# Two rounds of cached attention and MLP on one core: the queries of sixteen heads as products of 512 columns, wq in a bank of its own, output projections in 320 columns

## The chip, the cores and the metric

The kernel runs on one core of a Trainium2 chip, in one launch. The metric is the time of the program on the device in microseconds. Before the change three runs gave 711.83, 711.88 and 713.04 us, so the median is 711.88 us. The profile is that of one further execution; its span, from the first to the last instruction, is 710.5 us.

## The reference

x has four rows (B = 4) of 640 columns. Two rounds of the same two layers are computed, with the same weights and the same caches both times:

```python
# W = 1024: only the last 1024 of 4096 cache positions are used
def _A_ref(x, k_cache, v_cache, wq, wo):
    q = (x @ wq).reshape(4, 1, 32, 128).transpose(0, 2, 1, 3)
    scores = einsum("bhqd,bhkd->bhqk", q, k) * 128 ** -0.5
    p = softmax(scores, axis=-1)
    o = einsum("bhqk,bhkd->bhqd", p, v)
    return o.transpose(0, 2, 1, 3).reshape(4, 1, 4096) @ wo
def _B_ref(x, w1, w2):                     # w1 640 x 1728, w2 1728 x 640
    return maximum(x @ w1, 0) @ w2
x = x + _A_ref(layernorm(x), ...);  x = x + _B_ref(layernorm(x), ...)
x = x + _A_ref(layernorm(x), ...);  x = x + _B_ref(layernorm(x), ...)
```

Everything is float32. Each head has its own K and V for each of the four batch rows, so a head of a round needs 4 MB of cache for four rows of queries.

## The kernel before, in words

A column here is one float32 in each of the 128 partitions, 512 bytes. The host lays out one record per head in `rec`: 640 columns of wq, 4096 of K, 4096 of V and 640 of wo, together REC = 9472 columns (L48 to L51). The on-chip memory holds five records (`slots`, NS = 5, L128) and a `ring` of 9152 columns (L130). The ring takes the MLP weights (`w`, 17,280 columns a round), and most of record 26 (SIXTH, L62) stays in it or passes through it.

**Loads.** SP issues all loads from one list, `items`, which is written out at L209 to L245. `pump` (L247) issues the next piece when no part of its place is still `live`; `done` (L278) frees a part after the last product that reads it, and calls `pump`. So the list is strictly in order: a piece whose place isn't free holds up all behind it, and the DMA engines work only on what was issued before. In the steady part five records are cut into three pieces of some 15,800 columns (`stream`, L191).

**Work on a head.** `query` (L377) makes five products for a head: a 128x128 block of wq is the stationary side, four columns of x (transposed, `xT`) the moving side, and the result, scaled by the layernorm's deviation, is `qT`. `scores` (L388) makes eight products of 512 columns, `softmax` and `weights` turn them into the stationary side of `values` (L408), eight more products of 512 columns. `picks` (VectorE) and `output_T` bring the head's output into `oTs`, and `project` (L441) makes four products of 160 columns with wo, one for each quarter of the output, into `acc`, which is the residual x itself.

**Order.** The main loop (L500) writes the instructions of each engine in the order in which they are issued; the helper InOrder (L80) keeps it, so that nearly all instructions carry the helper's line L94. In the step of index n, `scores` of head n+1, `values` of head n, the query of head n+2, `output_T` and `project` of head n follow each other on TensorE. Round 0 takes the heads 0 to 31; round 1 takes 27 to 31, which are still in the slots, then 26 from the ring, then 0 to 25. At the start of a round `center` (L337) transposes x, and the first head's query is made from x that isn't centered: `centered_wq` (L327) has subtracted the mean from head 27's wq during the MLP of round 0. `deviation` follows inside the first `scores`. The start of round 1 is where the list has small pieces (L226 to L239), since only a part of the memory is free.

Of the kernel before, what the change touches and what calls it, by code (L numbers as in the profile page):

```python
# [22 lines left out]
WQ, K, V, WO = 0, D, D + 4 * W, D + 8 * W  # L48
REC = 2 * D + 8 * W
HALF = REC // 2  # L50
VH = 2 * W  # L51

# [9 lines left out]
SIXTH = H - NS - 1  # L62
RING = WO + 2 * FD
W1_COLS = KB * FF
KEPT = 4 * FF + 32
LENT = 512
BESIDE = KEPT - 192 - (512 - FD)
HELD = BESIDE - LENT

MLP_RING = [(4, 0, 0), (4, 0, FF), (4, 0, 2 * FF), (4, 0, 3 * FF), (4, 0, 0), (0, 10, 1728), (0, 11, 3328), (0, 11, 5088),  # L70
            (0, 10, 0), (0, 8, 1600), (0, 4, 2880)]

SIXTH_PIECES = [(3520, 5088), (5088, HELD), (0, 1600), (1600, 3520)]
FILL = [False, False, False, True]
W1_SLOT = [[0, 1], [2], [3], [4]]
W2_SLOT = [22, 14, 10, 4, 4]
LATE = 5

# [23 lines left out]
def decode_kernel(ctx: ExitStack, tc: tile.TileContext, xf, rec, w, out):  # L102
# [15 lines left out]
    qT = sb.tile([P, B], F32, name="qT")  # L118
    of_batch = sb.tile([P, B], F32, name="of_batch")
    of_block = sb.tile([P, 4], F32, name="of_block")  # L120
    pick = sb.tile([P, B], F32, name="pick")
    by_row = sb.tile([P, 2 * B], F32, name="by_row")
# [5 lines left out]
    slots = sb.tile([P, NS * REC], F32, name="slots")  # L128
    slot = [slots[:, i * REC:i * REC + REC] for i in range(NS)]
    ring = sb.tile([P, RING], F32, name="ring")  # L130
# [5 lines left out]
    acc = ps.tile([P, 512], F32, name="acc")  # L136
    outs = [o_ps, sc_ps[0][:, 512:]]

    dve.memset(x_sb, 0.0)
    for n in range(NB):  # L140
        act.dma_start(x_sb[32 * n:32 * n + B], xf[B * n:B * n + B])
    ident = ring[:, :P]
# [13 lines left out]
    dve.tensor_reduce(pick, same[:, :32].rearrange("p (c j) -> p j c", j=4), op=OP.add, axis=AX.X)  # L156
    dve.memset(small, EPS)
# [7 lines left out]
    LAST = H - NS  # L165
    order = [list(range(H)), list(range(LAST, H)) + [SIXTH] + list(range(SIXTH))]

    def home(h, r):

        if h == SIXTH:  # L170
            return "ring"
        return h % NS if not r or h >= LAST else (h + LAST) % NS
# [3 lines left out]
    at = {("rec", 1, SIXTH): [(0, RING, "ring", 0), (RING, REC, "ring", 0)]}  # L176
    live = []
    buffers = {"slots": slots, "ring": ring}

    def place(buf, col):  # L180
        return (buf, col) if buf == "ring" else ("slots", buf * REC + col)

    def load(key, src, lo, hi, buf, col):
        buf, col = place(buf, col)
        items.append(([(key, lo, hi, col)] if key else [], src, lo, hi, buf, col))

    def piece(r, h, lo, hi, buf=None, col=None):
        buf, col = place(home(h, r) if buf is None else buf, lo if col is None else col)
        items.append(([(("rec", r, h), lo, hi, col)], rec, h * REC + lo, h * REC + hi, buf, col))

    def stream(r, h, cuts):  # L191

        assert [home(h + i, r) for i in range(NS)] == list(range(NS))
        for a, b in zip(cuts, cuts[1:]):
            parts = [(("rec", r, h + i), max(a - i * REC, 0), min(b - i * REC, REC), max(a, i * REC))
                     for i in range(NS) if a < i * REC + REC and i * REC < b]
            items.append((parts, rec, h * REC + a, h * REC + b, "slots", a))
# [12 lines left out]
    piece(0, hs[0], 0, V)  # L210
    piece(0, hs[0], V, REC)
    stream(0, 0, [REC] + CUTS[1:])
    for h in range(NS, 5 * NS, NS):
        stream(0, h, CUTS)
    for h in hs[5 * NS:-3]:
        piece(0, h, 0, RING if h == SIXTH else WO if h >= H - LATE else REC)
    piece(0, SIXTH, RING, REC, "ring", 0)
    ending(0, hs, True)
    n = 0
    for quarters, tiles, col in MLP_RING:  # L220
        size = quarters * FQ + tiles * FD
        load(("w", 0), w, n, n + size, "ring", col)
        n += size


    for lo, hi in SIXTH_PIECES:  # L226
        load(None, rec[:, SIXTH * REC:], lo, hi, "ring", lo)
    new = order[1][NS + 1:]
    for i, lo, hi in ((0, 0, K), (0, K, K + VH), (0, K + VH, V), (1, 0, K + VH), (1, K + VH, V), (0, V, V + VH),
                      (0, V + VH, REC), (2, 0, V), (1, V, REC), (3, 0, V), (2, V, REC), (4, 0, V), (3, V, REC),  # L230
                      (4, V, REC)):
        piece(1, new[i], lo, hi)
    for h in new[NS:-3]:
        if h >= 2 * NS - 2:
            if home(h, 1) == 0:
                stream(1, h, CUTS)
        else:
            piece(1, h, 0, REC)
    ending(1, new, False)  # L239
    for ks in W1_SLOT:  # L240
        load(("w", 1), w, ks[0] * FF, (ks[-1] + 1) * FF, "ring", ks[0] * FF)
    n = W1_COLS
    for size in W2_SLOT:
        load(("w", 1), w, n, n + size * FD, home(new[-5], 1), n - W1_COLS)
        n += size * FD  # L245
# [32 lines left out]
    def done(key, lo, hi):  # L278

        if key[0] == "rec" and key[1] == 0 and key[2] >= LAST:  # L280
            return
        if key == ("rec", 0, SIXTH):
            hi = min(hi, HELD)
# [6 lines left out]
    aside = acc[:, FD:], ring[:, BESIDE:BESIDE + 512 - FD]  # L290
    held = [(0, 0, REC - RING), (REC - RING, BESIDE + 512 - FD, KEPT)]
    lent = sc_ps[1][:, :LENT], ring[:, HELD:BESIDE]

    def put_by():

        for col, a, b in held:
            dve.tensor_copy(hold[:, col:col + b - a], ring[:, a:b])
            free("ring", a, b)
        free("ring", BESIDE, KEPT)
        pump()  # L300

    def lend():

        act.activation(*lent, AF.Copy)
        free("ring", HELD, BESIDE)
        pump()

    def take_back():

        assert not any(buf == "ring" and x < BESIDE and HELD < y for buf, x, y in live), live  # L310
        act.activation(*lent[::-1], AF.Copy)
        live.append(("ring", HELD, BESIDE))

    def put_back():

        for col, a, b in held:
            assert not any(buf == "ring" and x < b and a < y for buf, x, y in live), (a, b, live)
            dve.tensor_copy(ring[:, a:b], hold[:, col:col + b - a])
            live.append(("ring", a, b))
        live.append(("ring", BESIDE, BESIDE + 512 - FD))  # L320
# [6 lines left out]
    def centered_wq(h, ks):  # L327

        mean = sc_ps[1][:, 512:512 + DH]
        for k in ks:  # L330
            pe.matmul(mean, minus.to_broadcast([P, P]), cols(("rec", 0, h), WQ + k * DH, DH), start=(k == 0),
                      stop=(k == KB - 1))
        if ks[-1] == KB - 1:
            wq = cols(("rec", 0, h), WQ, D).rearrange("p (k d) -> p k d", d=DH)
            dve.tensor_tensor(wq, wq, mean.unsqueeze(1).to_broadcast([P, KB, DH]), op=OP.add)

    def center(key=None, fill=True):  # L337

        x = acc[:, :FD]
        if key:  # L340
            q = sc_ps[0][:, :B]
            dve.transpose(xT[:, :64], x[:, :64])
            dve.transpose(xT[:, 64:], x[:, 64:])
            dve.tensor_reduce(sums, x, op=OP.add, axis=AX.X)
            for k in range(KB):
# [250 lines left out]
```

## Time and the profile before

| | us |
|---|---|
| median of three runs | 711.88 |
| lowest, highest | 711.83, 713.04 |
| span of the profiled execution | 710.5 |
| TensorE busy with products | 513.6 |
| VectorE busy | 323.3 |
| ScalarE busy | 99.7 |

The profiled execution's own time isn't given beside its span; the median of the runs is 1.4 us above that span, and this difference is used as what lies around it. The page names work by the program's tiles: `slots<-rec` is a load of record columns into the slots, `sc_ps<-slots,qT` a product of scores, `o_ps<-slots,scratch` one of values, `acc<-slots,oTs` one of the output projection, `sc_ps<-xT,slots` one of a query. Each product is counted as two matmul rows and two weight-load rows (992 rows of scores for 62 heads with eight products each). In the chain of waits a line has its start, its length and what it is; a DMA line is the time from the issue of a load to the moment when work that waited for it could start.

### The profile page before, as it was taken

To read this page: it belongs to the slowest core of one execution; us is meant where nothing else is said; L and a number is where in the kernel's file an instruction comes from. 1 tells how busy PE (TensorE), PEld (TensorE's weight loads), DVE (VectorE), ACT (ScalarE), POOL (GpSimd) and SP (SyncE) were. 2 spreads that over 40 slices of the span, in tenths; PEclk is the share of its full clock that TensorE was granted. 3 is DMA by queue.
4 is the path that set the end of the run, shared out by engine and by line. 5 is a ranking of instruction groups with operands and counts; after the bars stand their busy time and mean duration, and the time that the engine had idled before them with its cause. 6 is when DMAs were issued, how large, how long until landed. Compare 5 with 4: busy or idle time off the path is not lost.

```text
span 710.5 us, 8690 instructions
## 1 busy us (share of the span) xinstructions
PE 513.6 (72%) x3706; PEld 202.8 (29%) x3706; DVE 323.3 (46%) x678; ACT 99.7 (14%) x211; POOL 1.1 (0%) x9
## 2 busy tenths in 40 slices
PE   3567686678584578857888898865686677576897
PEld 2132232232231223322223334331331322231423
DVE  3333353353452353546641777644352444253762
ACT  1100110011010110111121212201010111011111
POOL 0000000000000000000000000000000000000000
PEclk9957787677777776888999899977576677677899
DMA  9999999999999999999999999999999999999997
GB/s 381 463 409 451 415 442 443 414 442 444 424 429 440 434 429 421 435 425 430 424 416 403 421 435 428 438 434 448 429 445 427 428 442 430 427 442 406 431 423 292
DMA packets 13318, 302.64 MB, mean 426 GB/s; under 512 B 1488, under 2 KB 1760, under 8 KB 5216
## 3 DMA queue, kind: packets, MB, share of 16 engines
q1 hardware_dynamic: 13248, 302.08, 99.1%
q8 instruction: 29, 0.48, 0.2%
q14 instruction: 9, 0.07, 0.0%
q10 hardware_dynamic: 32, 0.01, 0.0%
HBM read 302.00 MB, written 0.08 MB: 425 GB/s over the span
## 4 chain that ended last, share of the span: by engine, by line
DMA 73%; PE 21%; DVE 4%; issue 1%; ACT 1%; SPq 0%; ACTq 0%; DVEq 0%
DMA slots<-rec 57%; PE sc_ps L94 11%; DMA ring<-w 8%; PE o_ps L94 7%; DMA ring<-rec 5%; PE acc L94 2%; DMA slots<-w 2%; DVE scratch L94 2%; DVE o_ps L94 1%; ACT oTs L94 1%; DVE small L94 0%; ACT sc_ps L94 0%; DVE turned L94 0%; SPq L94 0%; DVE ring L94 0%
## 5 line engine op out<-in xcount | busy, mean ns | idle before, releaser
L94 PE MATMUL sc_ps<-slots,qT 128*4 128x512 f32 x992 | 194.5, 869 | 37.4 <-DMA slots<-rec 36.4
L94 PE MATMUL sc_ps<-xT,slots 128*128 128x4 f32 x620 | 94.6, 279 | 99.8 <-DMA slots<-rec 99.2
L94 PE MATMUL o_ps<-slots,scratch 128*16 128x512 f32 x960 | 149.3, 693 | 2.4 <-DVE scratch L94 1.7
L94 DVE TENSOR_REDUCE small<-sc_ps 128x1 f32<-128x1024 f32 x64 | 78.3, 1224 | 156.9 <-PE sc_ps L94 156.9
L94 PEld LDWEIGHTS sc_ps<-xT,slots 128*128 128x128 f32 x620 | 89.2, 225 | 157.8 <-DMA slots<-rec 109.0
L94 ACT ACTIVATE sc_ps<-sc_ps,small 128x1024 f32<-128x1024 f32 (+1 forms) x68 | 71.1, 1046 | 342.2 <-DVE small L94 340.7
L94 DVE STREAM_TRANSPOSE turned<-sc_ps 128x1024 f32<-128x1024 f32 (+1 forms) x85 | 84.6, 996 | 0.7
L94 PEld LDWEIGHTS o_ps<-slots,scratch 128*16 128x16 f32 x960 | 34.5, 118 | 120.0 <-issue 107.6
L94 DVE TENSOR_TENSOR o_ps<-o_ps,of_block 128x512 f32<-128x512 f32 x62 | 43.4, 699 | 53.6 <-PE o_ps L94 52.3
L94 PEld LDWEIGHTS sc_ps<-slots,qT 128*4 128x4 f32 x992 | 32.3, 108 | 121.9 <-issue 64.9
L94 DVE TENSOR_TENSOR qT<-sc_ps,by_row 128x4 f32<-128x4 f32 x62 | 9.7, 156 | 114.1 <-PE sc_ps L94 114.1
L94 PE MATMUL acc<-slots,oTs 128*4 128x160 f32 x496 | 35.4, 368 | 19.2 <-ACT oTs L94 18.5
L94 DVE TENSOR_REDUCE scratch<-o_ps 128x128 f32<-128x512 f32 x62 | 42.9, 691 | 2.1
L94 ACT ACTIVATE oTs<-o_ps 128x4 f32<-128x4 f32 x64 | 11.1, 174 | 214.1 <-PE o_ps L94 214.1
L94 PE MATMUL o_ps<-pick,scratch 128*128 128x4 f32 x128 | 26.8, 280 | 15.9 <-DVE scratch L94 15.9
L94 PEld LDWEIGHTS o_ps<-pick,scratch 128*128 128x128 f32 x128 | 22.4, 218 | 21.4 <-DVE scratch L94 21.1
L94 DVE TENSOR_TENSOR scratch<-turned,by_row 128x128 f32<-128x128 f32 (+1 forms) x85 | 22.0, 259 | 3.2
L94 PE MATMUL sc_ps<-slots,small 128*1 128x512 f32 (+2 forms) x56 | 21.5, 486 | 0.0
L94 DVE TENSOR_SCALAR by_row<-of_batch,small 128x4 f32<-128x4 f32 x64 | 14.7, 230 | 2.2
L94 PEld LDWEIGHTS acc<-slots,oTs 128*4 128x4 f32 x496 | 6.9, 84 | 25.2 <-ACT oTs L94 23.5
L94 DVE STREAM_TRANSPOSE scratch<-small 128x32 f32<-128x32 f32 x64 | 12.9, 202 | 2.2 <-ACT sc_ps L94 2.2
L94 ACT ACTIVATION_READ_ACCUMULATOR sc_ps<-sc_ps,small 128x1 f32 x64 | 12.3, 193 | 0.0
(66 smaller groups left out, 103.7 us busy)
## 6 DMA issues: line engine op xcount, KB each, us to landing
slots<-rec SPq DMA_DIRECT2D x15, 7872.0 KB, 27.0
slots<-rec SPq DMA_DIRECT2D x8, 7936.0 KB, 31.5
slots<-rec SPq DMA_DIRECT2D x17, 2368.0 KB, 16.9
slots<-rec SPq DMA_DIRECT2D x4, 4736.0 KB, 25.9
slots<-rec SPq DMA_DIRECT2D x2, 4416.0 KB, 29.3
slots<-rec SPq DMA_DIRECT2D x7, 1024.0 KB, 19.7
ring<-w SPq DMA_DIRECT2D x8, 864.0 KB, 10.9
ring<-rec SPq DMA_DIRECT2D x1, 4576.0 KB, 36.2
```

The costliest lines, as they stand in the source:

```text
L94: r = build(*args, **kwargs)
```

## The change

- wq leaves the records. REC is 8832 columns: K, V, wo. An array `wq` of two halves of 10,240 columns holds sixteen heads each; on the chip a half goes to `bank`, a tile of 10,240 columns. The slots get 1728 columns more (`extra`, from E0 on), the ring is gone, and the MLP weights of round 0 pass through `extra` and the fifth slot; those of round 1 go to the bank and the slots.
- `batch` makes the queries of sixteen heads: 20 products in which five columns of xT (four rows of x and one of ones) are the stationary side and 512 columns of wq the moving side. `turn` transposes the result on VectorE and applies mean and deviation. One batch stands at the start of each round, in `begin`, which replaces the first `center`; the other half's batch stands after the step of index 9 in round 0 and of index 3 in round 1 (BATCH). `query` and `centered_wq` are gone. The half that is used last in round 0 stays in the bank for the start of round 1; the other is loaded again.
- In 27 of 32 steps of round 0 and 24 of round 1, `project_wide` makes two products of 320 columns in place of four of 160. They go to `acc2`, and the last of a round adds it to `acc`.
- Round 1 takes 28 to 31, then 27 (FIFTH, of which a part stays in the fifth slot), then 0 to 26. Its list of loads after the small pieces goes on with the large pieces of `stream` at once, where there were three pieces of one record each before.

The loads, counted from the lists, are 589,824 columns before and 589,952 now, in as many DMAs.

```diff
-WQ, K, V, WO = 0, D, D + 4 * W, D + 8 * W
-REC = 2 * D + 8 * W
+K, V, WO = 0, 4 * W, 8 * W
+REC = 8 * W + D
+NQ = H // 2
+QB = KB * NB * 512
+LAST = H - NS + 1
+FIFTH = LAST - 1
+WIDE = [range(0, 27), range(4, 28)]
+BATCH = [9, 3]
...
-    ring = sb.tile([P, RING], F32, name="ring")
+    bank = sb.tile([P, QB], F32, name="bank")
...
+    queries(0, 0, 0, QB, "bank", 0)
+    stream(0, 0, [0, REC + V + 512, 3 * REC])
+    stream(0, 3, CUTS)
+    queries(0, 1, 0, QB, "bank", 0)
...
+    for i, j in ((3, 7), (7, 15), (15, 20)):
+        queries(1, 0, 512 * i, 512 * j, "bank", 512 * (i - 3))
...
-    for h in new[NS:-3]:
-        if h >= 2 * NS - 2:
-            if home(h, 1) == 0:
-                stream(1, h, CUTS)
-        else:
-            piece(1, h, 0, REC)
+    for h in (5, 10, 15):
+        stream(1, h, CUTS)
...
+    def batch(r, i, q, ks):
+        key = ("wq", r, i)
         for k in ks:
+            for j in range(NB):
+                pe.matmul(q[32 * j:32 * j + B + 1, :], xT[:, 32 * k:32 * k + B + 1], cols(key, 512 * (NB * k + j), 512),
+                          start=(k == 0), stop=(k == KB - 1))
+            done(key, 2048 * k, 2048 * k + 2048)
+
+    def turn(i, q, a, b):
+        dve.transpose(t_ps[:, 32 * a:32 * b], q[:, 32 * a:32 * b])
+        t = t_ps.rearrange("p (h j) -> p h j", j=32)[:, a:b]
+        n = b - a
+        dve.tensor_tensor(shift[:, a:b], t[:, :, B:B + 1].to_broadcast([P, n, B]),
+                          means.unsqueeze(1).to_broadcast([P, n, B]), op=OP.mult)
+        dve.tensor_tensor(qT[:, i, a:b], t[:, :, :B], rstds.unsqueeze(1).to_broadcast([P, n, B]), op=OP.mult)
+        dve.tensor_tensor(qT[:, i, a:b], qT[:, i, a:b], shift[:, a:b], op=OP.add)
+
+    def begin(r):
+        x, q, i = acc[:, :FD], sc_ps[1][:, 512:], r
+        dve.transpose(xT[:, :64], x[:, :64])
+        dve.transpose(xT[:, 64:], x[:, 64:])
+        dve.tensor_reduce(sums, x, op=OP.add, axis=AX.X)
+        batch(r, i, q, range(1))
+        pe.matmul(o_ps[:, :B], sums.to_broadcast([P, P]), first_rows, start=True, stop=True)
+        square(centered)
+        batch(r, i, q, range(1, 3))
+        deviation(eps_dh, float(DH))
...
+        batch(r, i, q, range(3, KB))
+        a = order[r][0] % NQ
+        turn(i, q, a, a + 2)
...
+    def project_wide(r, h, n):
+        key = ("rec", r, h)
+        for g in range(2):
+            pe.matmul(acc2[32 * g:32 * g + B, :], oTs[:, 0], cols(key, WO + g * (D // 2), D // 2),
+                      start=False, stop=(n == WIDE[r][-1]), skip_group_check=True)
...
-            query(r, hs[n + 2], n % 2)
             output_T(max(i, 0))
-            if i < 0:
+            if n in WIDE[r]:
+                project_wide(r, h, n)
+            elif i < 0:
                 project(r, h, 0, False)
...
+            if n == BATCH[r]:
+                batch(r, 1 - r, hold, range(KB))
+                turn(1 - r, hold, 0, NQ)
```

The first place is TensorE's start of round 1. Before, the last products of the MLP (`acc<-ring,scratch`) are followed by the query of head 27 and by its scores, with the mean and the deviation (`o_ps<-...small`) between them, and then by the first steps:

```order
L94 MATMUL acc<-ring,scratch 4x160 x12
L94 MATMUL sc_ps_72<-xT,slots 128x4 x5
L94 MATMUL o_ps<-pick,small 128x4
L94 MATMUL sc_ps_72<-slots,qT 4x512 x4
L94 MATMUL o_ps<-small 128x4
L94 MATMUL sc_ps_72<-slots,qT 4x512 x4
L94 MATMUL sc_ps_73<-xT,slots 128x4 x5
L94 MATMUL sc_ps_73<-slots,qT 4x512 x8
L94 MATMUL o_ps<-slots,scratch 16x512 x8
L94 MATMUL sc_ps_72<-xT,slots 128x4 x5
L94 MATMUL o_ps<-pick,scratch 128x4
L94 MATMUL acc<-slots,oTs 4x160 x4
```

Now the twenty products of a batch (`bank,xT`) stand ahead of the first scores, in the same place:

```order
L78 MATMUL acc<-slots,scratch 4x160 x12
L78 MATMUL sc_ps_77<-bank,xT 5x512 x4
L78 MATMUL o_ps<-first_rows,small 128x4
L78 MATMUL sc_ps_77<-bank,xT 5x512 x8
L78 MATMUL o_ps<-small 128x4
L78 MATMUL sc_ps_77<-bank,xT 5x512 x8
L78 MATMUL sc_ps_76<-slots,qT 4x512 x8
L78 MATMUL sc_ps_77<-slots,qT 4x512 x8
L78 MATMUL o_ps<-slots,scratch 16x512 x8
L78 MATMUL o_ps<-pick,scratch 128x4
L78 MATMUL acc<-slots,oTs 4x160 x4
```

The queries of the single heads have gone out of the steps, and twenty long products have come in ahead of them.

The second place is TensorE some steps later, after the step of index 3 of round 1. Now it reads, with the second batch (`turned<-...xT`) and the first wide projection:

```order
L78 MATMUL acc<-slots,oTs 4x160 x4
L78 MATMUL turned<-slots,xT 5x512 x3
L78 MATMUL turned<-bank,xT 5x512 x17
L78 MATMUL sc_ps_77<-slots,qT 4x512 x8
L78 MATMUL o_ps<-slots,scratch 16x512 x8
L78 MATMUL o_ps<-pick,scratch 128x4
L78 MATMUL acc<-slots,oTs 4x320 x2
```

Before, each step there is one of scores, values, query, `pick` and projection, as in the last five rows of the first fence. The second batch is in line ahead of all that follows it on TensorE.

The third place is SP's list of loads in round 1, from the end of the small pieces on. Before:

```order
L94 DMA slots<-rec 128x2048 x2
L94 DMA slots<-rec 128x2688
L94 DMA slots<-rec 128x4736 x7
L94 DMA slots<-rec 128x9472 x3
L94 DMA slots<-rec 128x15744
L94 DMA slots<-rec 128x15872
```

And now:

```order
L78 DMA slots<-rec 128x4736
L78 DMA slots<-rec 128x4096
L78 DMA slots<-rec 128x4736 x2
L78 DMA slots<-rec 128x14464
L78 DMA slots<-rec 128x14592
L78 DMA slots<-rec 128x15104
```

The three pieces of 9472 columns, one record each, are gone, and the first large piece, of 14,464 columns, follows a piece of 4736.

More of the change, by code (lines that the diff above doesn't have):

```diff
@@ L177, in decode_kernel @@
     live = []
[L178 to L189, printed above, removed]
+    buffers = {"slots": slots, "bank": bank}
@@ L191, in stream, with load, piece @@
+    def load(key, src, lo, hi, buf, col, first=0):
+        items.append(([(key, lo - first, hi - first, col)] if key else [], src, lo, hi, buf, col))
+    def piece(r, h, lo, hi):
+        load(("rec", r, h), rec, h * REC + lo, h * REC + hi, "slots", home(h, r) * REC + lo, h * REC)
     def stream(r, h, cuts):
-        assert [home(h + i, r) for i in range(NS)] == list(range(NS))
+        n, s = -(-cuts[-1] // REC), home(h, r)
+        assert [home(h + i, r) for i in range(n)] == list(range(s, s + n))
@@ L218, in decode_kernel @@
+    for h in (27, 28):
+        piece(0, h, 0, WO)
     ending(0, hs, True)
     n = 0
-    for quarters, tiles, col in MLP_RING:
+    for quarters, tiles, u in MLP_RING:
         size = quarters * FQ + tiles * FD
-        load(("w", 0), w, n, n + size, "ring", col)
+        load(("w", 0), w, n, n + size, "slots", at_ring(u))
         n += size
[L226 to L231, printed above, removed]
-        piece(1, new[i], lo, hi)
@@ L314, in put_back @@
     def put_back():
[L316 to L320, printed above, removed]
+        for there, a, b in held:
+            assert unused_by_loads(a, b), live
+            dve.tensor_copy(fifth[:, a:b], there)
+            live.append(("slots", BASE + a, BASE + b))
@@ L375, in xblock, with scores @@
         return xT[:, 32 * k:32 * k + B]
[L377 to L388 removed]
+    def scores(r, h, s):
         key = ("rec", r, h)
@@ L502, in decode_kernel @@
         late = LATE if r == 0 else 2
[L503 to L510 removed]
+        begin(r)
+        scores(r, hs[0], 0)
+        softmax(0)
         weights(0)
```

227 lines of the change are left out of this document (116 added, 111 removed).

## The prediction

> **What bounds the kernel now.** I read the page first, its chain's shares with it, then the stretches of the span, then the chain of waits in order of time.
>
> ```profile
> span 710.5 us, 8690 instructions
> PE 513.6 (72%) x3706; PEld 202.8 (29%) x3706; DVE 323.3 (46%) x678; ACT 99.7 (14%) x211; POOL 1.1 (0%) x9
> ...
> DMA packets 13318, 302.64 MB, mean 426 GB/s; under 512 B 1488, under 2 KB 1760, under 8 KB 5216
> ...
> q1 hardware_dynamic: 13248, 302.08, 99.1%
> q8 instruction: 29, 0.48, 0.2%
> ...
> DMA 73%; PE 21%; DVE 4%; issue 1%; ACT 1%; SPq 0%; ACTq 0%; DVEq 0%
> ```
>
> The load queue fills 99.1% of what sixteen DMA engines can do in the span. No engine of the core is above 72%. The time is the time of 302 MB, and the change can move it in three ways only: other bytes, a moment in which the loads have nothing to do, or the ends. The stretches (us, busy times of PE, PEld, DVE, ACT, POOL, the granted clock, the DMA share, GB/s) show where something is lost:
>
> ```profile
> 20.00:200.00 180.00, 124.44 (x766) 48.15 (x770) 69.59 (x137) 21.07 (x45) 0.00 (x0) 0.73 1.01 435
> ...
> 360.00:380.00 20.00, 16.50 (x162) 5.91 (x162) 5.21 (x15) 2.97 (x7) 0.00 (x0) 1.00 1.02 415
> 380.00:400.00 20.00, 16.93 (x159) 7.14 (x158) 8.68 (x27) 4.89 (x9) 0.00 (x0) 0.91 1.01 405
> 400.00:450.00 50.00, 44.39 (x376) 18.59 (x380) 36.55 (x78) 9.79 (x22) 0.00 (x0) 0.89 1.01 433
> 450.00:650.00 200.00, 138.58 (x946) 55.97 (x938) 85.61 (x167) 24.82 (x54) 0.00 (x0) 0.75 1.00 433
> ```
>
> In both steady stretches the engines move 433 to 435 GB/s at a share of 1.0; nothing is to be had there. At 433 GB/s, 1000 columns (512,000 bytes) take 1.18 us, and I use this throughout. At 380 to 400, where round 1 begins, 405 GB/s are 20 x 28/433 = 1.3 us lost. And TensorE is busiest beside full loads at 400 to 450: 44.39 of 50 us.
>
> **The part on bytes and on instructions.** The lists give 589,952 columns for 589,824: 128 columns, +0.15 us. The number of loads is the same. The instruction queue (q8) fetched 29 packets, and 29 x 256 = 7424 is the two rows of TensorE together, 2 x 3706 = 7412. The built programs have 1516 products for 1853, that is 2 x 2 x 1516 = 6064 rows, so 24 packets: five fewer. One is 0.48 MB/29 = 16.6 KB, 0.6 us on one engine at 433/16 = 27 GB/s. Spread over sixteen engines five are 0.2 us, all on the engine that ends last 3 us; I take -0.4, near the spread.
>
> **The steady part.** The work between the landing of a piece and the issue of the one that takes its place stands in the chain:
>
> ```profile
> 502.35 2.30 PE sc_ps L94 x10
> 504.65 0.44 PE o_ps L94 x2
> 505.18 0.18 ACT oTs L94
> 505.40 0.72 PE acc L94 x8
> 506.12 3.41 PE sc_ps L94 x16
> 509.53 2.30 PE o_ps L94 x16
> ...
> 514.11 0.76 PE acc L94 x8
> 514.88 24.74 DMA slots<-rec
> ```
>
> The first 2.30 us are a query's five products; they go, because qT is there long before. The two projections of four products took 0.72 and 0.76. No row shows two products of 320 columns on two column groups: the same columns on four groups side by side are the lower bound, 0.5 (a row below), one group after the other twice that at most, 1.5. I take 0.8, near the 0.76. So 514.88 - 502.35 = 12.5 us become 10 to 11. But the piece issued at 514.88, some 15,744 columns (18.6 us), landed 24.74 us later, so 6.1 us of other loads were queued ahead of it, and more now. Loads that are never out of work end no earlier: 0 us. The round 0 batch falls into this part: 4.3 to 8.5 us of products (below), and TensorE idles 55.6 of 180 us in the first stretch; the queue of 6.1 us covers what is left. Should that cover fail, it would cost at most 8.5 - 6.1 = 2.4 us once. At the program's start the first load is now 10,240 columns of wq ahead of any head; the lists need the first freed slot only behind 51,200 columns, 60 us. Taken at 0.
>
> **The start of round 1.** The small pieces up to the first record piece were 1568, 800, 1600 and 1920 columns, 5888; now 1440, 224, 1536 and 1920, 5120, before the first that waits for a batch. That is 768 columns or 0.9 us less in the queue where 1.3 us are lost already. So between -1.3 (the loss goes) and +0.9; I take 0, since what follows is freed by the first four products of the batch, about when the first query freed its wq.
>
> Then comes the place on which the forecast turns. In the chain:
>
> ```profile
> 385.60 0.26 DVE xT L94
> 385.90 1.28 PE sc_ps L94 x10
> ...
> 389.76 1.65 PE sc_ps L94 x8
> 391.43 1.24 DVE small L94
> ...
> 400.19 0.46 PE acc L94 x8
> ...
> 408.10 0.71 PE acc L94 x8
> ...
> 415.97 0.46 PE acc L94 x8
> ...
> 436.50 0.46 PE acc L94 x8
> 436.96 1.72 PE sc_ps L94 x16
> 438.67 1.76 PE o_ps L94 x16
> ...
> 442.71 0.50 PE acc L94 x8
> 443.23 18.13 DMA slots<-rec
> ```
>
> Here the loads wait for heads that were kept and that are worked off one after another: the projections of the indices 0, 5 and 6 stand at 400.19, 436.50 and 442.71, so steps take 36.3/5 = 7.3 us on average and 6.2 at the best. The query isn't in this chain: it ran while VectorE did the `picks`, so its removal shortens nothing here. What comes in is two batches. Eight products of 512 columns took 1.72 us at 436.96 and 3.41 at 506.12, so twenty take 4.3 or 8.5 us. The Trainium skill, in "TensorE: Matmul & The Clock Gate", Part 1, says that the array's clock has only a half and a full state, and goes to full after some 3.4 us of sustained work: by this estimate a batch begun cold does eight products in 3.4 us and twelve in 2.6, 6.0 in all. The two durations and the 2.30 us of values at 509.53, between 1.76 and twice that, agree with it.
>
> Before, scores end at 391.43. After, from 385.90: a batch of 4.3 to 8.5, `turn` on VectorE (five operations, taken at 1.0 from 0.26 for one at 385.60), scores of 1.72 to 3.41, so 392.9 to 398.8, 1.5 to 7.4 us later. The steps 1 to 5 take 5 x 6.2 = 31 to 5 x 7.9 = 39.5 us (7.9 is the first two, 400.19 to 408.10 to 415.97); behind step 3 the other batch, 4.3 to 8.5; its `turn` is beside the next scores on TensorE, 0. The list's first large piece, 14,464 columns, lies on head 0's place and on head 1's up to part of V, so it waits for the projection at index 5 and for the first half of the values at index 6: 0.5 + 1.72 + 0.9 to 0.5 + 3.41 + 1.2, 3.1 to 5.1 us. It is issued at 400.2 + 1.5 + 31 + 4.3 + 3.1 = 440 at the earliest, 400.2 + 7.4 + 39.5 + 8.5 + 5.1 = 461 at the latest, in the middle (400.2 + 4.5 + 36.3 + 6.4 + 4.1) 451.5.
>
> When do the loads run dry? Before, the piece of 9472 columns issued at 443.23 landed at 461.36, and 320,384 (round 0) + 5888 (the ring's part of record 26) + 56,832 (heads 0 to 5) = 383,104 columns had been loaded. After, 320,384 + 3584 (the part of record 27) + 10,240 (wq) + 44,160 (heads 0 to 4) = 378,368 lie ahead of the large piece, 4736 fewer: 5.6 us, so they are done by 455.8. The shortest load of the page gives the time from an issue:
>
> ```profile
> out<-scratch SPq DMA_DIRECT2D x1, 80.0 KB, 1.6
> ```
>
> So an issue by 455.8 - 1.6 = 454.2 costs nothing. The middle is 2.7 us ahead of it, the latest end 6.5 us behind. I take 0, with an upper end of 6.5. By the Trainium skill's 6.0 us a batch in place of 8.5 the latest end would be 5 us earlier and the stall at most 1.5.
>
> **The end.** The chain ends with loads of w and half a microsecond of products and of VectorE:
>
> ```profile
> 690.61 16.54 DMA slots<-w
> 707.19 0.50 PE acc L94 x8
> 707.72 0.33 DVE scratch L94
> ```
>
> The last pieces of w are the same in size and order: 0.
>
> **The sum.** 710.5 + 0.15 - 0.4 + 0 = 710.25 us of span; with the 1.4 us between the span and the median, 711.6 us. A measurement of this kernel tells some 0.2%, 1.4 us, from no change; so this is "the same".
>
> **The rivals.** First, slower: the large piece of round 1 is issued too late. Place: behind the second batch, at 454 to 461 on the trace's clock; it decides when the issue passes 454.2. From there every microsecond is the loads' own and goes whole to the end, since nothing later makes up for idle loads. For it: TensorE is busy 44.39 of 50 us here, two batches are added, the pieces of one record that could go out earlier are gone. Against: the middle of my sum is 2.7 us early, and the clock of 0.89 in this stretch is nearer to full. Price: 0 to 6.5, in the middle 3.2, so 714.8 us. The terms are long or short together, as one clock rules them; I count the range from 440 to 461 as even, of which 7 in 21 lie behind 454. The chance that it costs over 1.4 us is 0.34, less a little for stalls that are small and with the same again for what I put at 0 (the round 0 batch, the 0.9 us).
>
> Second, faster: the start of round 1 loses less, and the missing fetches count on the engine that ends last. For it: 405 GB/s there, and the wq for the kept heads no longer in the path. Against: fewer columns are queued there than before. Price: -1.3, and -1.0 beyond the -0.4 for fetches (of the 3 us that they are at the most), so 711.6 - 1.3 - 1.0 = 709.3 at the best and about 710.2 with half of it. Chance 0.15.
>
> Third, the loads of wq run slower than those of records, because of how its rows lie in memory: 30,720 columns are 36 us, and at half the rate 36 us are added, 748 us. Against it: w, an array of its own with short rows too, moved 415 GB/s at a share of 1.02 at 360 to 380. Chance 0.01. The Trainium skill, "DMA: Bandwidth & Descriptors", section "Latency and other measured facts", reports such a loss where the rows' distance is a large power of two, and that a pad of 192 bytes didn't help; wq's 20,672 columns a row are none, and no run here shows one.
>
> **How the numbers follow.** No stall and nothing gained: 0.50, at 711.6. Stalled: 0.34, 713.4 to 718. Faster: 0.15. wq slow: 0.01. The range leaves out the last, the stalls above five microseconds (about 0.10) and the better half of the faster case: 710.0 to 716.5. Chances: faster 0.15, same 0.50, slower 0.35.
>
> **What would show it.** Right: q1 at 99% or more, 433 GB/s in 450 to 650, q8 at 24 packets, and in the chain the piece of 14,464 columns issued before 454 with nothing of TensorE between it and loads that have run dry. The slower rival shows as a slice at 450 to 460 with a DMA share well under 1.0, and a chain which runs through both batches into that issue. The faster one shows as more than 405 GB/s at 380 to 400. A batch of twenty should take 4.3 to 8.5 us, and a pair of wide projections 0.5 to 1.5. Wrong would be an idle slice anywhere else, above all behind the batch of round 0, or fewer than 433 GB/s while wq is loaded.

## The result, and the profile after

The changed kernel takes 716.0 us (four runs, 715.3 to 717.49) where the kernel before took 711.96 beside it: a ratio of 1.0059, with a 95% interval of 1.0045 to 1.0073. It is slower by 4.0 us. The forecast was no change at 711.6; the range (710.0 to 716.5) holds the result, and the side on which the result lies had a chance of 0.35. But most of the loss is not the stall that this chance was given for. Single executions that took over 1.5% more than the fastest of their kernel, such as one of 1021.54 us in e1 and the profiled one of e13, are left out of the medians and comparisons below.

The page of the changed kernel, the rows that answer to those shown of before:

```profile
span 713.5 us, 7313 instructions
PE 436.5 (61%) x3032; PEld 112.6 (16%) x3032; DVE 322.6 (45%) x640; ACT 100.6 (14%) x213; POOL 1.1 (0%) x9
...
DMA packets 13313, 302.62 MB, mean 424 GB/s; under 512 B 1488, under 2 KB 1760, under 8 KB 4960
...
q1 hardware_dynamic: 13248, 302.14, 99.1%
q8 instruction: 24, 0.39, 0.2%
...
DMA 68%; PE 23%; DVE 6%; issue 1%; another core or an unknown queue 1%; ACT 1%; SPq 0%; DVEq 0%; ACTq 0%
```

TensorE has 77 us less work and five fetches are gone, as counted. The load queue (q1) has the same 13,248 packets and 0.06 MB more, and the same share, 99.1%, of a span that is 3.0 us longer. That is the first thing to read: its packets (a packet is one piece of a load, in one partition) fill 0.991 x 713.5 = 707.1 us on each engine instead of 0.991 x 710.5 = 704.1, and 6.4 us are left empty in both. The durations of the single packets in the two traces, added up, say the same: 706.9 and 704.0 us. The loads did not wait more in this execution. They took longer.

The stretches of the changed kernel, in the same columns as before:

```profile
20.00:200.00 180.00, 102.46 (x630) 24.09 (x626) 71.19 (x135) 22.32 (x47) 0.00 (x0) 0.77 1.00 433
...
360.00:380.00 20.00, 16.23 (x144) 4.40 (x143) 5.36 (x16) 3.44 (x8) 0.00 (x0) 1.00 1.02 406
380.00:400.00 20.00, 15.66 (x178) 4.58 (x174) 6.98 (x27) 3.56 (x6) 0.00 (x0) 1.00 1.01 395
400.00:450.00 50.00, 35.33 (x286) 9.53 (x282) 32.30 (x68) 8.29 (x18) 0.00 (x0) 0.90 1.01 428
450.00:650.00 200.00, 114.89 (x742) 29.52 (x734) 90.19 (x159) 27.48 (x60) 0.00 (x0) 0.83 1.00 433
```

The rate falls where the pieces are small: 415 to 406 at 360 to 380, where the MLP's weights come, and 433 to 428 behind the change of the rounds. In the long pieces it is the same. A price that goes with the number of packets, not with the bytes, looks like this. The 405 to 395 at the change of the rounds says less: other executions of the kernel before, shown below, have up to 413 there.

The forecast stall isn't there. In the chain of waits of this execution the second batch and the first large piece of round 1, with the projections of the indices 0 and 5, are:

```profile
403.81 0.45 PE acc L78 x8
...
427.93 4.52 PE turned L78 x40
...
446.34 0.70 PE acc L78 x2
...
451.21 23.45 DMA slots<-rec
```

The piece was issued at 451.21, where the middle of the forecast was 451.5, and landed 23.45 us later; its own 14,464 columns are 17.1 us, so 6.4 us of loads were still ahead of it.

So three theories went into the runs. **A, the place:** the tiles of this kernel lie in each partition one behind the other. The built programs put the slots at byte 3072 and the ring at 192,512 before, both multiples of 256, and the slots at 3648 and the bank at 187,200 after, both 64 bytes past one, because qT has grown by 480 bytes and three small tiles of 32 bytes each stand ahead of them (below). A load that writes off such a multiple would then take longer. **B, the work beside the loads:** the longer products read the memory that the loads write to, and slow them. **C, the gap of the forecast:** the first large piece comes too late, in executions other than the one profiled. Later there is also **D:** the loads run short at the change of the rounds. The lines of the change behind theory A, ahead of the slots' allocation:

```diff
-    qT = sb.tile([P, B], F32, name="qT")
+    qT = sb.tile([P, 2, NQ, B], F32, name="qT")
...
+    first_rows = sb.tile([P, B], F32, name="first_rows")
+    halves = sb.tile([P, 2, B], F32, name="halves")
+    means = sb.tile([P, B], F32, name="means")
```

### The profile page after: what moved, and what is told of

Same layout as the page of the kernel before. It is cut to its first block, busy times and chain, and to the rows that moved or that the text cites. A ratio compares the mean times of both kernels' runs of the same rounds, so it can differ in the third digit from the quotient of the medians.

```text
span 713.5 us, 7313 instructions
## 1 busy us (share of the span) xinstructions
PE 436.5 (61%) x3032; PEld 112.6 (16%) x3032; DVE 322.6 (45%) x640; ACT 100.6 (14%) x213; POOL 1.1 (0%) x9
## 3 DMA queue, kind: packets, MB, share of 16 engines
q1 hardware_dynamic: 13248, 302.14, 99.1%
## 4 chain that ended last, share of the span: by engine, by line
DMA 68%; PE 23%; DVE 6%; issue 1%; another core or an unknown queue 1%; ACT 1%; SPq 0%; DVEq 0%; ACTq 0%
DMA slots<-rec 63%; PE sc_ps L78 11%; PE o_ps L78 9%; DMA slots<-w 6%; DVE scratch L78 2%; PE acc L78 2%; DVE o_ps L78 2%; PE turned L78 1%; DVE turned L78 1%; ACT oTs L78 0%; DVE small L78 0%; DVE slots L78 0%; ACT sc_ps L78 0%; DVE sc_ps L78 0%
## 5 line engine op out<-in xcount | busy, mean ns | idle before, releaser
L78 PE MATMUL o_ps<-slots,scratch 128*16 128x512 f32 x992 | 164.1, 682 | 7.1 <-DVE scratch L78 6.5
L78 DVE STREAM_TRANSPOSE turned<-sc_ps 128x1024 f32<-128x1024 f32 (+3 forms) x88 | 86.3, 980 | 3.0 <-PE sc_ps L78 2.4
L78 PE MATMUL acc<-slots,oTs 128*4 128x320 f32 (+1 forms) x308 | 46.8, 425 | 20.2 <-ACT oTs L78 19.5
L78 PEld LDWEIGHTS o_ps<-slots,scratch 128*16 128x16 f32 x992 | 39.9, 112 | 115.6 <-issue 108.2
L78 PEld LDWEIGHTS o_ps<-pick,scratch 128*128 128x128 f32 x128 | 19.2, 189 | 156.9 <-DVE scratch L78 155.7
L78 PE MATMUL sc_ps<-slots,small 128*1 128x512 f32 (+1 forms) x50 | 22.8, 552 | 0.0
L78 PE MATMUL sc_ps<-bank,xT 128*5 128x512 f32 (+1 forms) x120 | 17.9, 703 | 0.7 <-DVE xT L78 0.7
L78 PE MATMUL acc<-slots,scratch 128*4 128x160 f32 x224 | 10.2, 299 | 4.9 <-DMA slots<-w 4.7
L78 DVE RECIPROCAL small<-scratch 128x1 f32<-128x1 f32 x64 | 10.5, 164 | 2.2
```

Source lines behind the costliest of these rows:

```text
L78: r = build(*args, **kwargs)
```

## The experiments

**e1: the changed kernel on multiples of 256.** The slots and the bank are allocated ahead of `small`; no instruction changes.

```diff
+    slots = sb.tile([P, NS * REC + EXTRA], F32, name="slots")
+    bank = sb.tile([P, QB], F32, name="bank")
     small = sb.tile([P, 16], F32, name="small")
...
-    slots = sb.tile([P, NS * REC + EXTRA], F32, name="slots")
...
-    bank = sb.tile([P, QB], F32, name="bank")
```

> The changed kernel with one allocation moved: the 64 bytes of `small` lie behind the bank, so that the slots begin at 3584 bytes in each partition and the bank at 187,136, multiples of 256, where they began at 3648 and 187,200, 64 past such a multiple. No instruction changes. Theory A (the place): the same 13248 packets of loads each take a few nanoseconds longer when what they write begins off a multiple of 256 bytes, and this is the loss; then the time falls by 2.5 to 3.5 us, to 712.5 to 713.5, and the span to 710 to 711. Theory B (the work beside the loads): the longer products of the changed kernel slow the loads down by reading the same memory; then nothing changes, 716. Theory C (a gap): the loads run dry somewhere in round 1; then nothing changes either, 716.

713.1 us, a ratio to before of 1.0016, interval 1.0007 to 1.0024. 2.9 of the 4.0 us are gone. The stretches at 20 to 200, 360 to 380, 380 to 400 and 400 to 450 us now read:

```profile
20.00:200.00 180.00, 103.67 (x630) 24.32 (x626) 71.19 (x134) 22.24 (x47) 0.00 (x0) 0.77 1.00 434
360.00:380.00 20.00, 16.07 (x156) 4.91 (x156) 4.46 (x14) 2.97 (x7) 0.00 (x0) 1.00 1.01 411
380.00:400.00 20.00, 15.61 (x167) 4.14 (x166) 7.72 (x29) 3.55 (x6) 0.00 (x0) 1.00 0.99 385
400.00:450.00 50.00, 35.32 (x270) 9.45 (x266) 31.29 (x66) 8.27 (x18) 0.00 (x0) 0.86 1.01 431
```

411 for 406 and 431 for 428, so the rate comes back where the pieces are small; but not at 380 to 400 (385), which is what D goes after. The packets add up to 704.8 us an engine, 2.1 less than on the old places. Packets of equal length took 2 to 3 ns less each by the median of the trace's records: 262 for 265 ns those of 6,912 bytes, 611 for 613 those of 16,384, 2154 for 2156 those of 58,368.

**e2 and e3: the kernel before, 64 and 128 bytes off.** A tile of 64 or 128 bytes that nothing uses is put ahead of the slots.

```diff
+    sb.tile([P, 16], F32, name="gap")
     slots = sb.tile([P, NS * REC], F32, name="slots")
 # e3: the same, with 32 for 16
```

> The kernel before with a gap of 64 bytes ahead of the slots, so that slots and ring begin 64 bytes past a multiple of 256 (3136 and 192,576) where they began at multiples (3072 and 192,512). Nothing else changes. Theory A: slower by 2 to 3.5 us, 714 to 715.5. Theories B and C: no change, 712.

> The kernel before with a gap of 128 bytes, slots and ring 128 past a multiple of 256. Theory A with 256 bytes as the unit: slower by 2 to 3.5 us as with 64. Theory A with a smaller unit (128 or 64 would do): no change, 712, in the case of 64 in the run with 64 too. Theories B and C: no change.

715.04 us (1.0043, 1.0030 to 1.0056) and 714.67 us (1.0039, 1.0027 to 1.0051): the kernel before, with the same instructions, loses 3.3 and 2.9 us. The page with 64 bytes, and its stretch at 360 to 380 us, where 415 GB/s had been:

```profile
span 713.3 us, 8690 instructions
...
q1 hardware_dynamic: 13248, 302.08, 99.0%
```

```profile
360.00:380.00 20.00, 16.68 (x150) 5.69 (x149) 7.27 (x19) 3.57 (x8) 0.00 (x0) 1.00 1.02 402
```

The packets of the trace add up to 706.4 us an engine for 704.0: 2.4 us. Of the 13,248 packets 1472 have 4 bytes each and take 9 ns in both; over the other 11,776/16 = 736 an engine the 2.4 us are 3.3 ns each on average. By the median it is again 2 to 3 ns at most lengths (265 for 262 ns at 6,912 bytes, 2326 for 2324 at 62,976), with 128 bytes as with 64. At 380 to 400 us both runs have 413 GB/s for the 405 of before: that stretch doesn't show the place.

**e8, a control: 256 bytes lower.** The slots at 2816 and the ring at 192,256, odd multiples of 256, with small tiles behind them.

```diff
+    sb.tile([P, 16], F32, name="gap")
+    slots = sb.tile([P, NS * REC], F32, name="slots")
+    ring = sb.tile([P, RING], F32, name="ring")
     oTs = sb.tile([P, LATE, B], F32, name="oTs")
...
-    slots = sb.tile([P, NS * REC], F32, name="slots")
...
-    ring = sb.tile([P, RING], F32, name="ring")
```

> The kernel before with slots and ring 256 bytes lower (2816 and 192,256, odd multiples of 256), the small tiles from oTs on behind them, and a gap of 64 bytes. A control: if the unit is 256 bytes, no change, 711.5 to 712.3; if it is 512, slower by 2 to 3.5 us; if any move of the tiles costs time, slower too.

711.89 us, 1.0002 (0.9993 to 1.0011), and its span:

```profile
span 709.9 us, 8690 instructions
...
q1 hardware_dynamic: 13248, 302.08, 99.1%
```

No change. So it isn't the move: 2816 and 3072 cost nothing, 3136 and 3200 do, and 256 bytes are a unit that is enough. The Trainium skill, "DMA: Bandwidth & Descriptors", section "How a descriptor splits into AXI transactions", says of a transfer that doesn't begin at a multiple of 256 bytes that its first transaction begins at the multiple below, and that the bytes fetched ahead of its start are unused and still cost time. The four places agree with 256 as the unit; but what the page tells is told of bytes that are fetched, and what was moved here is where the loads write. Why that costs 2 to 3 ns, and no more with 128 bytes than with 64, the runs don't show.

**e4: projections in 160 columns again.** Theory B's likeliest form:

```diff
-WIDE = [range(0, 27), range(4, 28)]
+WIDE = [range(0), range(0)]
```

> The changed kernel with all output projections as four products of 160 columns again (the two lists of wide ones are empty); batches and places as in the changed kernel. Theory A: no change, 715.5 to 716.5, or as much as the instruction fetches cost (0.2). Theory B, if the wide projections are what disturbs: 712 to 713.5. Theory C: not better, since each step is as long or longer, 716 to 717.

716.1 us, 1.0069 (1.0053 to 1.0085): not faster. B falls for the projections, and with e2, where the old products lose as much, for the rest. What this run shows beside that is theory C. The chain of its profiled execution, which took 717.42 us, at the second batch and the large piece, and its stretch at 450 to 460 us:

```profile
429.78 6.22 PE turned L78 x40
...
455.95 19.71 DMA slots<-rec
```

```profile
450.00:460.00 10.00, 7.13 (x60) 2.22 (x64) 6.73 (x13) 1.55 (x4) 0.00 (x0) 0.83 1.04 418
```

Here the batch took 6.22 us, the large piece went out at 455.95, and it landed only 2.6 us later than its own 17.1 us need. 418 GB/s stand where the changed kernel's profiled execution had 462 in this stretch:

```profile
450.00:460.00 10.00, 6.54 (x56) 1.87 (x48) 7.13 (x12) 2.59 (x5) 0.00 (x0) 1.00 1.08 462
```

The stretch's share, 1.04, doesn't show a gap, since a packet counts where it starts. The packet records do: added up over the time in which fewer than sixteen packets were under way, the engines stood idle for at least 0.9 us each on average between 455 and 458; none such time is found from 450 to 460 in the changed kernel's profiled execution. So the stall of the forecast exists, in some executions, at about the time that was given as its limit (454).

**e5: the first large piece cut.** On the places of e1:

```diff
-    for h in (5, 10, 15):
+    stream(1, 5, [0, REC] + CUTS[1:])
+    for h in (10, 15):
         stream(1, h, CUTS)
```

> The changed kernel with the places on multiples of 256 (as in e1_aligned), and the first large piece of round 1 cut where its first record ends: 8832 columns that need only the projection of index 5, then 5632 that need the values of index 6. One load more. What is still lost against the kernel before is 1.5 us. Theory C (that piece is issued too late): 712.0 to 713.0, with the first of the two pieces issued some 3 us earlier than 452. Theory D (the loss is at the change of the rounds, where the first 1536 columns of wq are issued about 1 us before the loads run dry): no change, 713.0 to 713.5.

712.97 us, 1.0011 (1.0002 to 1.0020), 0.1 us better than e1 by the medians and 0.4 by the ratios, with intervals that overlap: at most a small part of what was left is C.

**e11 and e12: the second batch left out, and made twice.** Both on the places of e1; the first leaves out the products and the `turn` for heads 0 to 15 in round 1.

```diff
 # left out
             if n == BATCH[r]:
-                batch(r, 1 - r, hold, range(KB))
-                turn(1 - r, hold, 0, NQ)
+                if r:
+                    done(("wq", r, 1 - r), 0, QB)
+                else:
+                    batch(r, 1 - r, hold, range(KB))
+                if r == 0:
+                    turn(1 - r, hold, 0, NQ)
 # twice: the same products as in batch, without its done
             if n == BATCH[r]:
+                if r:
+                    twice(r, 1 - r, hold)
                 batch(r, 1 - r, hold, range(KB))
```

> The changed kernel with the places on multiples of 256, and the second batch of round 1 left out, products and turn alike; its wq is loaded as before and the heads 0 to 15 of round 1 use the queries of round 0. Theory C (the first large piece of round 1 is late because of that batch, in part of the executions): the piece is issued 4 to 5 us earlier than at 452, and the time falls by what C costs, 0 to 0.6 us from 713.1, to 712.5 to 713.1. If C costs more than I think: under 712.5.

> The changed kernel with the places on multiples of 256, and the twenty products of the second batch of round 1 made twice, with the same result. It puts 4.3 to 5 us more on TensorE ahead of the first large piece's release. Theory C with the deadline as forecast, issue by 454: the piece is issued at 456 to 458 and the time rises by 2 to 4 us, to 715 to 717. If the loads had more in hand there than I think: no change, 713.

Without it 712.87 us (1.0014, 1.0005 to 1.0023), and the piece goes out at 444.95; e1 had it at 452.30. With it twice 715.2 us (1.0045, 1.0026 to 1.0064). The chain rows of the piece, without and with twice the products:

```profile
444.95 28.16 DMA slots<-rec
```

```profile
423.59 8.81 PE turned L78 x80
...
449.63 23.77 DMA slots<-rec
```

Without the batch 11 us of loads are in hand and 0.2 us are gained, within the noise: this piece is not what limits e1. With twice the products the seven runs lie between 712.54 and 717.82, wider than in any other kernel here. The profiled execution took 712.88: its clock was granted in full at 400 to 450 us, where e1 had 0.86, so that the step before and the step after the batch were short and the piece went out earlier than in e1.

```profile
400.00:450.00 50.00, 35.34 (x332) 10.11 (x324) 32.58 (x67) 8.27 (x18) 0.00 (x0) 1.00 1.01 431
```

The expectation of an issue at 456 to 458 was thus wrong for this execution, and that of 2 to 4 us more right in the median. That the longer ones are those with less clock there is argued, not shown: only their clock over the whole execution is on record, which is 0.833 and 0.835 in the two longest and 0.839 to 0.847 in the others.

**e6 and e7, the change of the rounds: finer pieces.** Theory D. On the places of e1, the last ten-tile load of w, the 1536 columns of wq and the 1920 of record 27 are each cut in two.

```diff
-            (0, 10, 0), (0, 8, 1728), (0, 4, 3008)]
+            (0, 5, 0), (0, 5, 800), (0, 8, 1728), (0, 4, 3008)]
...
-    queries(1, 0, 0, 3 * 512, "slots", E0)
+    queries(1, 0, 0, 512, "slots", E0)
+    queries(1, 0, 512, 3 * 512, "slots", E0 + 512)
...
-    load(None, rec, FIFTH * REC + lo, FIFTH * REC + hi, "slots", BASE + lo)
+    for lo, hi in ((lo, lo + 1280), (lo + 1280, hi)):
+        load(None, rec, FIFTH * REC + lo, FIFTH * REC + hi, "slots", BASE + lo)
```

> The changed kernel with the places on multiples of 256, and finer pieces at the change of the rounds: the load of ten tiles of w whose place the wq columns take is cut into five and five, the 1536 columns of wq into 512 and 1024, the 1920 columns of record 27 into 1280 and 640, so that each can go out as soon as its own part of the place is free. Three loads more. Theory C: no change, 713.0 to 713.5. Theory D: 712.2 to 712.8, and the stretch at 380 to 400 us with 395 GB/s or more in place of 385.

> The changed kernel with the places on multiples of 256 and both sets of finer pieces. If C and D each hold in part, 711.5 to 712.3, no slower than the kernel before; if neither, 713.0 to 713.5.

713.98 us (1.0034, 1.0021 to 1.0048), and with e5's cut as well 714.03 (1.0031, 1.0020 to 1.0042). Both miss what either theory expected: worse than e1 by 0.9. The stretch in e6 had fallen to 376 GB/s, and to 371 in e7:

```profile
380.00:400.00 20.00, 15.39 (x158) 4.66 (x160) 7.22 (x27) 3.55 (x6) 0.00 (x0) 0.98 0.97 376
```

The profiled execution of e6 took 716.13 us, the longest of its five; that of e7, 714.03, is its median. The remedy failed; it doesn't tell whether the place is right. So the queue itself was changed, in both kernels, by order alone.

**e9, e10, e13 and e14: fewer columns queued at that wait.** In the kernel before (e9), 704 columns go behind the 1600 that wait for w's last products; as a control (e10) the same cut without the move; then (e13) all 2368 columns behind them, without a cut. In the kernel of e5 (e14) the 1536 columns of wq go ahead of 1664 others.

```diff
 # e9, e10, e13: the kernel before
-SIXTH_PIECES = [(3520, 5088), (5088, HELD), (0, 1600), (1600, 3520)]
+SIXTH_PIECES = [(3520, 5088), (5088, 5184), (0, 1600), (5184, HELD), (1600, 3520)]
+SIXTH_PIECES = [(3520, 5088), (5088, 5184), (5184, HELD), (0, 1600), (1600, 3520)]
+SIXTH_PIECES = [(0, 1600), (3520, 5088), (5088, HELD), (1600, 3520)]
 # e14: the kernel of e5
+    queries(1, 0, 0, 3 * 512, "slots", E0)
     lo, hi = FIFTH_PIECES[0]
...
-    queries(1, 0, 0, 3 * 512, "slots", E0)
```

> The kernel before with 704 columns of the ring moved in SP's list from ahead of the 1600 columns that wait for w's last products to behind them (800 columns cut into 96 and 704), so that as little is queued there at the change of the rounds as in the changed kernel. One load more, the same columns. Theory D (the loss that is left in the changed kernel is what is missing in the queue at the change of the rounds): slower by 0.5 to 1.0 us, 712.2 to 712.7, and fewer GB/s than 405 at 380 to 400 us. If D is false: no change, 711.6 to 711.9.

> A control for e9_before_late: the same cut of 800 columns into 96 and 704, both where the 800 were. One load more. Theory D, with the order as what counts: no change or the price of one load, 711.7 to 712.0. If the number of loads is what costs there, the same as e9_before_late.

> The kernel before with the 1600 columns that wait for w's last products moved in SP's list ahead of the 1568 and 800 columns that are free earlier; the same loads in another order. 2368 columns, 2.8 us, are missing in the queue while that piece waits. Theory D (what is queued ahead of this wait sets the loss at the change of the rounds): slower by 1.5 to 2.5 us, 713.2 to 714.3, with under 390 GB/s at 380 to 400 us. If D is false: no change, 711.6 to 712.0.

> The changed kernel as in e5_cut (places on multiples of 256, first large piece cut), with the 1536 columns of wq moved in SP's list ahead of the 1440 and 224 columns of record 27; the same loads in another order. 1664 columns, 2.0 us, are missing in the queue while that piece waits, and it had nothing in hand. Theory D: slower than e5_cut by 1.5 to 2.0 us, 714.4 to 715.0. If D is false: no change, 712.9.

712.37 us (1.0007, 0.9998 to 1.0015) against 711.98 (1.0005, 0.9996 to 1.0014): 0.4 us, inconclusive. With 2368 columns 712.76 (1.0010, 1.0001 to 1.0019): 0.9 us, less than expected; of this kernel no stretch can be compared. In the changed kernel 714.87 (1.0041, 1.0028 to 1.0055): 1.9 us more than e5 for 1664 columns, which are 1.96 us. The stretch there:

```profile
380.00:400.00 20.00, 15.71 (x164) 4.25 (x166) 8.30 (x29) 3.55 (x6) 0.00 (x0) 0.94 0.92 357
```

A missing 2.8 us cost the kernel before 0.9, so by this reckoning it had about 1.9 us in hand at that wait; a missing 1.96 us cost the changed kernel 1.9, so it had nothing in hand. That is theory D, and it is shown as far as this goes. It doesn't price the changed kernel's own deficit by itself. The stretch does, roughly. In the four executions on multiples of 256 that leave this place as it is it has 385 GB/s (e1, above), 390 (e5), 401 (e11) and 393 (e12); the kernel before has 405, and 413 in e8. The rows of e5, e11, e12 and e8:

```profile
380.00:400.00 20.00, 15.69 (x164) 4.14 (x166) 7.88 (x29) 3.55 (x6) 0.00 (x0) 1.00 0.99 390
380.00:400.00 20.00, 15.69 (x164) 4.16 (x166) 8.13 (x29) 3.55 (x6) 0.00 (x0) 0.98 1.01 401
380.00:400.00 20.00, 15.55 (x164) 4.14 (x166) 7.87 (x29) 3.55 (x6) 0.00 (x0) 1.00 1.01 393
380.00:400.00 20.00, 17.06 (x163) 7.27 (x166) 8.94 (x28) 5.02 (x9) 0.00 (x0) 0.91 1.02 413
```

The four are 392 on average, which is 20 x 13/433 = 0.6 us against 405; e1 alone is 0.9, and against 413 the average would be 1.0.

The packet records, counted as in e4, say how much of this is idle time of the engines: at least 0.14 us in the kernel before at 380 to 400, 0.56 in e1, 0.45 in e5, 0.2 in e11 and e12, 1.0 in e6 and e7, and 2.0 in e14. So the queue does run empty here, by 1.6 us more in e14 than in e5, and the finer pieces of e6 left it emptier. But of the 0.9 us of e1 only 0.4 are idle time more than before. The rest is packets that took longer in this stretch, which no run here explains, and in the changed kernel's own profiled execution the idle time is 0.17.

## Why the prediction was wrong, point by point

**Bytes and fetches** held as counted: 128 columns more, 24 fetches. **The step that failed stands there, and isn't a number in it:** "the number of loads is the same", and from that and the columns their time, at 433 GB/s "throughout". The loads' own duration was no term of the sum and had no bounds, although the diff enlarges qT and adds tiles ahead of the slots, so that every load of records writes elsewhere. Measured, that term is 2.9 us in the changed kernel (716.0 to 713.1) and 2.9 to 3.3 in the kernel before. That the result lies in the range all the same is luck: the range was made for a stall. The third rival (the loads of wq run slower because of their rows in memory) was a relative of it, at the other end of the transfer and for one array only; wq's packets of 40,960 bytes took 1514 ns in the median of e1, 27 GB/s an engine, as fast as the others. The trace of before could not show the price; the two built programs show only that slots and ring lay on multiples of 256 and that slots and bank no longer did.

**The steady part** held: 433 GB/s at 450 to 650, and the chain from landing to issue is shorter. In the changed kernel it is 8.3 us (579.27 to 587.60), less than the 10 to 11 forecast:

```profile
579.27 3.52 PE sc_ps L78 x16
582.79 1.77 PE o_ps L78 x16
584.66 0.71 DVE o_ps L78
585.39 0.70 DVE scratch L78
586.14 0.40 PE o_ps L78 x2
586.85 0.44 PE acc L78 x2
587.60 26.93 DMA slots<-rec
```

The forecast took out the query's 2.30 us alone. What left the chain with it is the 1.5 us of the head before (its `output_T` and projection, 504.65 to 506.12); from the scores on it was 8.8 us (506.12 to 514.88) and is 8.3. The clock doesn't explain the difference to the forecast: the scores took 3.52 us, the slow one of the two durations. The chain's being shorter gave nothing, as forecast. A wide pair took 0.44 here; the 0.8 was too much, and so was its bound of 1.5, which isn't twice 0.5, as the prediction has it, but about twice the 0.76 of a projection.

**The start of round 1** was given -1.3 to +0.9 and taken at 0, because the next pieces would follow in time. It is on the upper side: 0.6 to 1.0 by the stretch, so this term was mis-sized too. That the 0.9 us counted as missing in the queue had no cover is what e14 shows.

**The first large piece**: the mechanism and the place were right, and its price in the median was small. The changed kernel had 451.21 for the forecast 451.5, and that close it is by luck: the projection of index 0 came at 403.81, 0.9 before the middle of the sum, the way from there to that of index 5 took 38.0 us beside the batch for 36.3, the batch 4.52 for 6.4, and the rest 4.9 for 4.1. The limit of 454 fits e4, whose piece was issued at 455.95 with 0.9 us of idle engines behind it; but the 1.6 us in the limit came from the row `out<-scratch`, which is the store of the result and no load. The runs of e12 lie 5.3 us apart, and that this is the same stall is argued. On good places C is worth 0.1 to 0.4 us (e1 against e5), within the noise. The batch took 4.52 us in the changed kernel and in e7, and 6.22 in e1, e4, e5, e6 and e14; in e1 the granted clock was 0.51 for 3.4 us of it, and half of that is the 1.7 us of difference. The 6.0 worked out from the Trainium skill's "TensorE: Matmul & The Clock Gate", Part 1, which wasn't taken for the sum's end, was nearer than the 8.5 that was.

**The sum**, then, of what the runs give: 2.9 for the place, 0.6 to 1.0 for the change of the rounds, 0.1 to 0.4 for the large piece, 0.15 for the bytes, together 3.8 to 4.5 of 4.0; the last two lie within the noise of a comparison. What stays open is how the 0.6 to 1.0 are shared between fewer columns in the queue, w's products coming later and the longer packets there, and no version here beats the kernel before: e5, the best of those that leave no work out, is at 712.97.

## What to carry to other kernels

Where loads set the time, look at where in a partition each large tile begins whenever tiles are added or grow ahead of it, and keep the large ones on multiples of 256 bytes, the small tiles behind them; here two allocations in another order gave 2.9 us. When the bytes and the queue's share (here 99%) stay and the span grows, the packets themselves have become slower: divide the difference by their number before looking for a gap. And at a wait that has nothing in hand, a microsecond missing in the queue is one on the end (1.9 for 1.96 in e14), while a wait with some in hand takes part of it for nothing (0.9 for 2.8 in e13); the order of the list alone can test which of the two it is.

## What the runs showed of the hardware that was not expected

A begin 64 or 128 bytes off a multiple of 256 makes a load packet 2 to 3 ns longer by the median and 3.3 ns on average (e2), nearly independent of its length: 2 ns of 2324 in packets of 63 KB, 3 of 262 in those of 6.9 KB, where the rate falls by 3% (415 to 402 GB/s). Two kernels with equal instructions differ by 3.3 us for it.

Twice the products in the batch made one execution of e12 no longer, with the clock at 1.00 around them, for 0.86 in e1. The Trainium skill, "TensorE: Matmul & The Clock Gate", Part 1, says that sustained work is what raises the clock. This trace can't show that the added products did it, since the clock was full from 400 us on and the batch began at 423.59; and seven runs between 712.54 and 717.82 show that it can't be counted on.
